# Feed-forward weights issued right behind the last query projection and no longer one by one; one stationary tile for both halves of each down product

## The chip, the cores and the metric

One core of one Trainium2 chip. The time is the device time of an execution in microseconds. PE is TensorE, PEld its weight loads, ACT ScalarE, DVE VectorE, SP the engine that issues most DMAs, in program order. "Half clock" is a stretch in which the records show TensorE's granted clock at 0.5.

## The reference, cut to what matters

A memory-augmented recurrent attention over 64 segments of 32 tokens, then a gated feed-forward. Everything is bfloat16; tokens 2048, width 640, 32 heads of 128, feed-forward width 1728.

```
for s in range(64):                       # each segment needs the memory rows of the one before
    h = concat([mem, x[32*s : 32*s+32]])
    q, k, v = h @ Wq, h @ Wk, h @ Wv
    o = softmax(mask(q k^T * scale)) v @ Wo
    mem = o[:8]; outs.append(o[8:])
h  = x + concat(outs)
n  = layernorm(h)
h2 = h + (relu(n @ W_gate) * (n @ W_up)) @ W_down
```

## The kernel before

A small dependency tracker turns read and write keys into semaphore waits. A write to a key waits for the key's last writer *and* for all its readers since. SP works through its DMAs in program order and blocks at the first that has to wait.

SBUF is nearly full. The gate weights (Wg), the up weights (Wu), their remainder (Wgu, 2 x 64 columns) and the first block of normalized rows (xn2T) take the place of the query weights; Wd, the down weights, and the rows `h` take that of the key weights. `("Wdone", j)` is a key that each projection with weight matrix j writes.

```python
def load_gate_up():
    free = [("W", 0, 0), ("W", 0, 1)]                 # the query weights' keys
    dma(xn2T[0], xn2_d, r=[...] + [("Wdone", 0)], w=[...])
    for n, (t, src) in enumerate(((Wg, B_W_gate), (Wu, B_W_up))):
        dma(t, src[..., 0:FM],             w=free + [(("Wg", "Wu")[n],)])   # each writes `free`,
        dma(Wgu[..., n*FR:(n+1)*FR], src[..., FM:F], w=free + [("Wgu", n)]) # so waits for the last
# ... (cut)
for s in range(NSEG):
    # project K; P.V of segment s-1; project Q (not in the last); project V; scores; softmax  (cut)
    v_riders(par, t0, nr)          # copies of 24 token rows of V between partitions, by DMA
    if s == NSEG - 2:
        load_gate_up()
    # attention output, Wo pass, the attention rows' stores  (cut)
# hand-over: last segment's rest, mixed with gate_up(0, 0..3) on PE
dma(h_rows[0], h_d, ...)
dma(Wd[:, 0:FC-1, :], ..., w=[("W", 1, 0), ("W", 1, 1), ("Wd", 0)])
dma(Wd[FR:128, FC-1, :], ..., w=[("W", 1, 0), ("W", 1, 1), ("Wd", 1)])
for i in range(4, 8): ln2_load(i)                     # eight loads of x and attention rows
trans_ox(s-1); wo_pass(...); rows(...)                # rows: ACT copies to wtok, SP stores it
gate_up(0, 0); pv_x(s); gate_up(0, 1); trans_ox(s); wo_pass(...); rows(...); gate_up(0, 2) # ... (cut)

def down(b, u):                                        # one 128-token tile; contraction 13 x 128 + 64
    for hf in range(2):
        for j in range(FC):                            # FC = 14; the last tile has 64 rows
            p0 = 0 if j < FC - 1 else FR
            pe.matmul(bank(BD[hf])[:, 0:320], hT[par][p0:128, j, u*128:(u+1)*128],
                      Wd[p0:128, j, hf*320:(hf+1)*320], start=(j == 0), stop=(j == FC - 1))
        # DVE: osb = bank + h_rows
```

The softmax here doesn't subtract the row's maximum and nothing guards it: scores larger than these inputs give would overflow.

## Time and profile before

| | before |
|---|---|
| time at the prediction | 1268.34 us, median of 3 (1266.53 to 1270.35) |
| profiled span | 1262.6 us |
| last query projection ends | 1026.65 us |
| first down product starts | 1101.51 us |
| 112 down matmuls of a block, first to last start | 16.72 us |

The page of before, its span, PE's busy share and the chain of work that ended last by engine:

```profile
span 1262.6 us, 64636 instructions
...
PE 1176.5 (93%) x31431; PEld 661.4 (52%) x29111; DVE 611.0 (48%) x1497; ACT 408.4 (32%) x775; POOL 26.6 (2%) x94
...
PE 86%; DMA 4%; DVE 4%; ACT 3%; issue 1%; SPq 1%; POOL 0%; DVEq 0%; ACTq 0%; POOLq 0%
```

PE is the bottleneck, and 4% of the chain is DMA, half of it the loads at the start. The rest lies in the hand-over. The timeline of before, SP's DMA issues there (start, duration of the issue, what is loaded from what):

```profile
1033.95 0.43 SPq L304 DMA_DIRECT2D Wg<-in_B_W_gate_dram  x1
1044.24 0.38 SPq L304 DMA_DIRECT2D Wgu<-in_B_W_gate_dram  x1
1046.34 0.37 SPq L304 DMA_DIRECT2D Wu<-in_B_W_up_dram  x1
1055.37 0.37 SPq L304 DMA_DIRECT2D Wgu<-in_B_W_up_dram  x1
...
1057.96 11.35 SPq L304 DMA_DIRECT2D Wd<-in_B_W_down_dram  x2
...
1075.04 6.17 SPq L304 DMA_DIRECT2D attn_d<-wtok  x12
```

Each weight goes out when the one before has landed; the twelve attention stores stand behind the second piece of Wd. What PE and ACT pay, from the timeline of before (in brackets the idle time ahead of the line and what ended it):

```profile
1055.49 2.29 PE L884 MATMUL ps<-xn2T,Wu 128*128 128x512 bf16 x5 [4.24 <-DMA Wu<-in_B_W_up_dram]
...
1079.37 0.30 ACT L378 ACTIVATE wtok<-ps 128x160 bf16<-128x160 f32 x1 [12.69 <-DMA attn_d<-wtok]
...
1080.22 1.25 PE L884 MATMUL ps<-xn2T,Wg 128*128 128x512 bf16 x5 [3.14 <-ACT g L897]
```

PE's weight loads in a down group, from the timeline of before:

```profile
1248.25 1.85 PEld L912 LDWEIGHTS ps<-Wd,hT 64*128 64x128 bf16 x14 [0.26 <-issue]
...
1250.36 1.85 PEld L912 LDWEIGHTS ps<-Wd,hT 64*128 64x128 bf16 x14 [0.26 <-issue]
```

A group of 14 takes 2.11 us, and there is one break in it, ahead of the 64-row tile.

### The profile page before, as it was taken

What the parts mean: (1) busy time and instruction counts of PE and PEld (TensorE: products, weight loads), DVE (VectorE), ACT (ScalarE), POOL (GpSimd) and SP (SyncE); (2) the same over time, 40 slices, a digit from 0 to 9 for tenths busy, and PEclk for the clock granted to TensorE, in tenths of its full rate; (3) what the DMA queues carried; (4) which work ended last, traced back from release to release, by engine and by line L of the source; (5) the groups of instructions that cost most, each with busy time, mean ns of one, the idle gap of its engine ahead of it and who ended that gap; (6) DMA issues with size and microseconds to landing.
All of it is one profiled execution on the core that took longest, in us unless ns stands there. A gap on an engine that the chain in (4) does not pass through costs nothing.

```text
span 1262.6 us, 64636 instructions
## 1 busy us (share of the span) xinstructions
PE 1176.5 (93%) x31431; PEld 661.4 (52%) x29111; DVE 611.0 (48%) x1497; ACT 408.4 (32%) x775; POOL 26.6 (2%) x94
## 2 busy tenths in 40 slices
PE   0889999999999999999999999999999997999998
PEld 0255555555556555555555555555555554455454
DVE  2244545454545454555555555454545442543522
ACT  0323333333333333333333333333333321321311
POOL 1000000000000000000000000000000000000000
PEclk9999999999999999999999999999999998999999
DMA  9801000010110101010111010100000025110100
GB/s 364 310 21 24 21 23 21 23 23 22 23 24 21 25 19 25 21 44 19 43 22 44 21 44 20 24 20 23 20 21 20 19 99 183 37 63 22 43 21 21
DMA packets 47819, 60.03 MB, mean 48 GB/s; under 512 B 20224, under 2 KB 36288, under 8 KB 47552
## 3 DMA queue, kind: packets, MB, share of 16 engines
q1 hardware_dynamic: 43520, 45.41, 12.6%
q10 hardware_dynamic: 4032, 10.49, 2.2%
q8 instruction: 237, 3.88, 1.3%
q14 instruction: 30, 0.25, 0.1%
HBM read 36.79 MB, written 6.55 MB: 34 GB/s over the span
## 4 chain that ended last, share of the span: by engine, by line
PE 86%; DMA 4%; DVE 4%; ACT 3%; issue 1%; SPq 1%; POOL 0%; DVEq 0%; ACTq 0%; POOLq 0%
PE ps L345 32%; PE ps L546 12%; PE ps L331 9%; PE ps L884 9%; PE ps L364 6%; PE ps L912 5%; PE ps L488 3%; PE ps L372 2%; PE ps L558 2%; PE ps L521 2%; DVE TBf L466 2%; DMA W<-in_A_Wk_dram 2%; PE ps L583 2%; ACT Kr L378 1%; ACT Qr L378 1%
## 5 line engine op out<-in xcount | busy, mean ns | idle before, releaser
L345 PE MATMUL ps<-W,act_r 128*32 128x512 bf16 x6460 | 447.2, 381 | 39.0 <-DVE act_r L467 12.6
L345 PEld LDWEIGHTS ps<-W,act_r 128*32 128x32 bf16 x6460 | 162.9, 96 | 286.0 <-issue 84.4
L380 DVE CAST tok<-ps 128x512 bf16<-128x512 f32 x161 | 110.9, 689 | 154.8 <-PE ps L345 78.3
L378 ACT ACTIVATE tok<-ps 128x512 bf16<-128x512 f32 x161 | 95.9, 596 | 229.7 <-PE ps L331 187.8
L546 PE MATMUL ps<-Wo,oT 128*32 128x160 bf16 x8448 | 163.8, 236 | 3.1 <-issue 2.6
L546 PEld LDWEIGHTS ps<-Wo,oT 128*32 128x32 bf16 x8448 | 148.6, 98 | 12.7 <-issue 4.5
L331 PE MATMUL ps<-W,act_r 128*32 128x512 bf16 x1420 | 138.8, 381 | 0.0
L364 PEld LDWEIGHTS ps<-ident,tok 128*128 128x128 bf16 x1288 | 72.2, 98 | 48.5 <-issue 24.2
L364 PE MATMUL ps<-ident,tok 128*128 128x128 bf16 x1288 | 89.1, 220 | 4.7 <-DVE tok L380 4.7
L604 ACT ACTIVATE oT<-ps 128x768 bf16<-128x768 bf16 x64 | 51.9, 811 | 124.4 <-PE ps L372 124.4
L345 PE MATMUL ps<-W,act_e 128*32 128x512 bf16 x900 | 89.6, 381 | 0.1
L331 PE MATMUL ps<-W,act_e 128*32 128x512 bf16 x900 | 89.2, 379 | 0.0
L378 ACT ACTIVATE Qr<-ps 128x512 bf16<-128x512 bf16 (+3 forms) x110 | 69.1, 658 | 57.4 <-DVE Qr L380 45.4
L596 DVE TENSOR_TENSOR ox<-ps,rx 128x512 bf16<-128x512 f32 x128 | 82.4, 685 | 2.2
L899 DVE TENSOR_TENSOR hT<-g,ps 128x512 bf16<-128x512 bf16 (+1 forms) x56 | 37.8, 686 | 74.7 <-PE ps L884 53.1
L466 DVE STREAM_TRANSPOSE TBf<-ps 128x160 f32<-128x160 f32 x64 | 22.4, 350 | 100.7 <-PE ps L546 100.6
L884 PE MATMUL ps<-xn2T,Wu 128*128 128x512 bf16 x260 | 66.7, 388 | 4.2 <-DMA Wu<-in_B_W_up_dram 4.2
L884 PE MATMUL ps<-xn2T,Wg 128*128 128x512 bf16 x260 | 66.6, 388 | 3.1 <-ACT g L897 3.1
L912 PE MATMUL ps<-Wd,hT 128*128 128x320 bf16 x448 | 68.1, 300 | 0.0
L378 ACT ACTIVATE wtok<-ps 128x160 bf16<-128x160 f32 x64 | 19.5, 304 | 138.7 <-DVE TBf L466 122.4
L897 ACT ACTIVATE g<-ps 128x512 bf16<-128x512 f32 (+1 forms) x56 | 32.3, 594 | 97.1 <-PE ps L884 97.1
L380 DVE CAST Vp<-ps 128x512 bf16<-128x512 f32 x64 | 44.3, 692 | 27.8 <-PE ps L345 26.4
(88 smaller groups left out, 1169.5 us busy)
## 6 DMA issues: line engine op xcount, KB each, us to landing
Vr<-Vp SPq DMA_DIRECT2D x124, 48.8 KB
xt<-in_A_x_dram SPq DMA_DIRECT2D x30, 160.0 KB
Vr<-Vp SPq DMA_DIRECT2D x128, 32.5 KB
attn_d<-wtok SPq DMA_DIRECT2D x256, 7.5 KB
W<-in_A_Wk_dram ACTq DMA_DIRECT2D x1, 2560.0 KB
W<-in_A_Wq_dram ACTq DMA_DIRECT2D x1, 2560.0 KB
W<-in_A_Wv_dram ACTq DMA_DIRECT2D x1, 2560.0 KB
Wo<-in_A_Wo_dram ACTq DMA_DIRECT2D x1, 2560.0 KB
```

Of the source, the lines that this page charges most:

```text
L331: return pe.add_instruction(mybir.InstMatmult(name=nc.get_next_instruction_name(), engine=mybir.EngineType.PE, ins=[pe.lower_ap(rhs), pe.l ...
L345: ins = pe.matmul(*a, start=(c == 0), stop=(c == DC - 1), skip_group_check=True)
L364: ins = pe.matmul(bank_bf(b)[:, k * 128:(k + 1) * 128], t[:, (k % 4) * 128:(k % 4 + 1) * 128], ident[:, :], is_transpose=True)
L378: add("act", lambda a: a.activation(dst, src, ACTF.Copy), r=r, w=w)
L380: add("dve", lambda v: v.tensor_copy(dst, src), r=r, w=w)
L466: add("dve", lambda v: v.transpose(TBf[:].rearrange("p c t -> p (c t)"), src), r=[wkey], w=[("TBf",)])
L488: i = pe.matmul(o, lh, Qr[:, h, q, :], start=True, stop=True, skip_group_check=True)
L546: i = pe.matmul(bank(bk)[32 * gg:32 * gg + 32, 0:160], src[:, hb, :], w[:, gg], start=(hb == 0), stop=(hb == 31), skip_group_check=True)
L596: add("dve", lambda v, kh=kh: v.tensor_tensor(ox[:, :, kh, :], src[:, :, kh, 0:128], ap(rx, kh, [[2, 4], [0, 128]]), ALU.mult), r=[B(b0 + ...
L604: add("act", lambda a: a.activation(oT[par][:, :, M:32].rearrange("p (k g) q -> p g k q", g=4), src[:, :, :, 0:RID], ACTF.Copy), r=[B(bk)] ...
L884: ins = pe.matmul(bank(bk), w[:, c, lo:lo + 128], xn2T[par][:, c, :], start=(c == 0), stop=(c == DC - 1))
L912: i = pe.matmul(bank(bk)[:, 0:320], hT[par][p0:128, j, u * 128:(u + 1) * 128], Wd[p0:128, j, hf * 320:(hf + 1) * 320], start=(j == 0), sto ...
```

## The change

Three parts: the four gate and up weight DMAs wait for the last query projection alone and not for one another, likewise the two of Wd for the last key projection; the gate and up fetch moves from behind segment 62's softmax to right behind its query projection; the two halves of a down product share each stationary tile (`again` issues a matmul without a weight load), in bank pairs that alternate.

```diff
 def load_gate_up():
-    free = [("W", 0, 0), ("W", 0, 1)]
+    free = [("Wdone", 0)]
...
-        dma(t, ..., w=free + [(("Wg", "Wu")[n],)])          # and Wgu alike
+        dma(t, ..., r=free, w=[(("Wg", "Wu")[n],)])
...
             if not last:
                 project(a, ks, 0, (0, 1), (P0, P1))
+                if s == NSEG - 2:
+                    load_gate_up()
...
-        if s == NSEG - 2:
-            load_gate_up()
...
-    dma(Wd[...], ..., w=[("W", 1, 0), ("W", 1, 1), ("Wd", 0)])   # second piece alike
+    dma(Wd[...], ..., r=[("Wdone", 1)], w=[("Wd", 0)])
...
 def down(b, u):
-    for hf in range(2): for j in range(FC): matmul(bank(BD[hf]), hT[j], Wd[j, hf])
+    bks = (BD, BT)[u % 2]
+    for j in range(FC):
+        p0 = 0 if j < FC - 1 else FR
+        for hf in range(2):
+            if hf and not p0: again(pe, ...)                 # no weight load
+            else:             pe.matmul(...)                 # the 64-row tile loads twice
```

More of the change, by code (lines that the diff above doesn't have):

```diff
@@ L327, in build_kernel, with again @@
     nq = [0]
-    def again(pe, dst, lhsT, rhs, start, stop, g):
+    def again(pe, dst, lhsT, rhs, start, stop, g, size=(128, 32)):
         return pe.add_instruction(mybir.InstMatmult(
@@ L333, in again @@
             ins=[pe.lower_ap(rhs), pe.lower_ap(lhsT)], outs=[pe.lower_ap(dst)], start_tensor_calc=start,
-            stop_tensor_calc=stop, tile_size=(128, 32), tile_position=(0, 32 * g), bass_skip_group_check=True, ldweights=False))
+            stop_tensor_calc=stop, tile_size=size, tile_position=(0, 32 * g), bass_skip_group_check=True, ldweights=False))
     def project(act, akeys, j, halves, banks, chunks=range(5)):
@@ L713, in load_gate_up @@
         for n, (t, src) in enumerate(((Wg, B_W_gate), (Wu, B_W_up))):
-            dma(t[:, :, :], src.rearrange("(c p) f -> p c f", p=128)[:, :, 0:FM], w=free + [(("Wg", "Wu")[n],)])
+            dma(t[:, :, :], src.rearrange("(c p) f -> p c f", p=128)[:, :, 0:FM], r=free, w=[(("Wg", "Wu")[n],)])
             dma(Wgu[:, :, n * FR:(n + 1) * FR], src.rearrange("(c p) f -> p c f", p=128)[:, :, FM:F],
-                w=free + [("Wgu", n)])
+                r=free, w=[("Wgu", n)])
     PARTS = ((0, 1), (2, 3), (4,))
@@ L905, in down, with f @@
         n_o[0] += 1
-        for hf in range(2):
-            bk = BD[hf]
-            for lo, hi in ((0, FC - 2), (FC - 2, FC)):
-                def f(pe, hf=hf, bk=bk, lo=lo, hi=hi):
-                    for j in range(lo, hi):
-                        p0 = 0 if j < FC - 1 else FR
-                        i = pe.matmul(bank(bk)[:, 0:320], hT[par][p0:128, j, u * 128:(u + 1) * 128],
-                                      Wd[p0:128, j, hf * 320:(hf + 1) * 320], start=(j == 0), stop=(j == FC - 1))
-                    return i
-                add("pe", f, r=[("hT", par, j) for j in range(lo, hi)] + [("Wd", 0), ("Wd", 1)], w=[B(bk)])
+        bks = (BD, BT)[u % 2]
+        for lo, hi in ((0, FC - 2), (FC - 2, FC)):
+            def f(pe, lo=lo, hi=hi):
+                for j in range(lo, hi):
+                    p0 = 0 if j < FC - 1 else FR
+                    for hf in range(2):
+                        a = (bank(bks[hf])[:, 0:320], hT[par][p0:128, j, u * 128:(u + 1) * 128],
+                             Wd[p0:128, j, hf * 320:(hf + 1) * 320])
+                        if hf and not p0:
+                            i = again(pe, *a, j == 0, j == FC - 1, 0, (128, 128))
+                        else:
+                            i = pe.matmul(*a, start=(j == 0), stop=(j == FC - 1), skip_group_check=True)
+                return i
+            add("pe", f, r=[("hT", par, j) for j in range(lo, hi)] + [("Wd", 0), ("Wd", 1)], w=[B(k) for k in bks])
+        for hf in range(2):
+            bk = bks[hf]
             add("dve", lambda v, hf=hf, bk=bk: v.tensor_tensor(osb[o][:, hf * 320:(hf + 1) * 320], bank(bk)[:, 0:320],
@@ L925, in build_kernel @@
     dma(Wd[:, 0:FC - 1, :], B_W_down[0:FM, :].rearrange("(j p) d -> p j d", p=128),
-        w=[("W", 1, 0), ("W", 1, 1), ("Wd", 0)])
-    dma(Wd[FR:128, FC - 1, :], B_W_down[FM:F, :], w=[("W", 1, 0), ("W", 1, 1), ("Wd", 1)])
+        r=[("Wdone", 1)], w=[("Wd", 0)])
+    dma(Wd[FR:128, FC - 1, :], B_W_down[FM:F, :], r=[("Wdone", 1)], w=[("Wd", 1)])
     for i in range(4, 8):
```

## The prediction

> **What bounds the kernel now.** The page of before: span 1262.6 us, PE busy 93%, the chain that ended last 86% PE. Up to 1030 us that is the attention recurrence, which the change does not touch. It touches two places.
>
> *1. The hand-over to the feed-forward, 1030 to 1085 us.* The chain of waits there is made of DMA. In the timeline SP issues Wg at 1033.95, the next piece at 1044.24, Wu at 1046.34, the last at 1055.37: each write to the same tracking key waits for the landing before it (SP waits: 9.8 us for Wg, 8.7 for Wu). The last query projection, which frees their space, ends at 1026.9. PE pays three times:
> - Gate product 0 is done at 1051.1; PE idles 4.24 us for Wu.
> - The clock records then grant half speed from 1054.3 to 1061.1 (windows: 0.75 over 1056 to 1066). The five Wu products take 2.2 us, not 1.08; the next Wg five the same.
> - Wd's second piece waits 10.3 us for the first in the SP queue, so twelve attention stores go out only at 1075 to 1081. ACT idles 12.7 us for one of them (a wtok buffer), until 1079.37; its relu comes late and PE idles 3.14 us "<-ACT g" before 1080.22. More half clock follows (1081.6 to 1085.0).
>
> *2. The down products.* Four blocks of 112 matmuls take 16.88 us each, 150.7 ns per matmul, at clock 1.00. Start to start most are 135.8 ns, the weight load hidden. The excess is at the last, 64-row tile: 232 ns into it, 238 out of it, 147 for the next, about 0.21 us per group of 14. This agrees with "Mode switching requires drain" (the Trainium skill, TensorEngine Tiling (Array Packing), Key Properties).
>
> **What the change does.** The weights are issued from about 1027.0, when SP has finished its stores, within 2.5 us. The queue moved about 400 GB/s at its peaks, so 5.1 MB should land near 1042, before 1050. The 62nd segment's V rider copies now stand behind them (descriptors are consumed in ring order: DMA: Bandwidth & Descriptors, HWDGE ordering), landing near 1044 by this estimate; they are needed at 1052. Wd goes out near 1041, lands near 1055, is needed past 1085. The attention stores go out near 1050 and land near 1056; ACT needs that at about 1062.
>
> PE then runs Wu at 1051.1, the value product to 1052.95, gate/up 1 to 1055.1. Before, that point was 1061.9: 6.8 us saved. The ACT stall goes, 3.3 us, and the half clock behind it, 1.7 us. Sum 11.8 us, all on the critical path.
>
> Down: dropping 208 of 448 weight loads saves nothing by itself, since they are hidden. But both halves now share one visit to the 64-row tile: 16 groups instead of 32, 16 x 0.21 = 3.4 us. Both evictions now follow the last matmul: the tail grows by one, 0.5 us. Net 2.9 us.
>
> **Prediction.** 1268.3 - 11.8 - 2.9 = 1253.6 us. 8 in 10: 1249.5 to 1258. Faster by over 2%: 0.03; within 2%: 0.96; slower: 0.01.
>
> **What would show it.** No PE wait on DMA Wu; clock 1.00 from 1038 us to the end; no ACT wait over 1 us for an attention store; 112 down matmuls in about 16.0 us, still 136 ns apart; half as many slow steps; PE idle between segments 62 and 63 (om, ox) unchanged.
>
> **What would make it wrong.** Rider copies or stores held behind 9 MB of weights, so that the value product of segment 63 or ACT waits; instruction fetch slowed by the full DMA (two PE gaps of 0.4 to 0.6 us marked "issue" stand here already); a matmul without weight load not streaming at 136 ns.

## More of the kernel before

The stage windows of before, with the granted clock (PEclk), the DMA engines' share and their GB/s. The rows are: query projection to gate product 0; to the last transposes of the attention output; to gate/up 5; to the first down product; one block of down products.

```profile
core 0: us, PE busy (x) PEld busy (x) DVE busy (x) ACT busy (x) POOL busy (x), PEclk, DMA share, GB/s
1026.65:1050.00 23.35, 18.81 (x631) 13.29 (x623) 8.43 (x22) 6.27 (x11) 0.00 (x0) 0.93 0.48 163
1050.00:1061.93 11.93, 7.69 (x89) 2.85 (x86) 2.18 (x4) 1.50 (x3) 0.00 (x0) 0.71 0.62 211
1061.93:1080.22 18.29, 14.59 (x360) 9.18 (x358) 1.67 (x3) 2.54 (x6) 0.00 (x0) 1.00 0.58 182
1080.22:1101.51 21.29, 21.29 (x106) 9.79 (x107) 14.17 (x30) 8.71 (x21) 0.00 (x0) 0.92 0.02 4
1101.51:1118.40 16.89, 16.89 (x115) 10.24 (x112) 4.82 (x9) 1.47 (x3) 0.00 (x0) 1.00 0.09 30
```

The second stage is a third idle and runs at 0.71 of the clock. The down stage is full at full clock; the reader has to look at single starts to see anything there.

## The result, and the profile after

| | before | after |
|---|---|---|
| time, fast runs of the first set | 1267.65 us (4 runs) | 1257.28 us (4 runs) |
| ratio, 95% interval | | 0.9916 (0.9898 to 0.9934) |
| control, second set | 1266.28 us (11 runs) | 1258.89 us (6 runs) |
| ratio, 95% interval | | 0.9940 (0.9918 to 0.9962) |

A ratio compares two kernels in the same set and is not quite the ratio of the medians quoted; a gain in microseconds is here 1 minus the ratio, times the median of before in that set. The gain is 10.6 us by the first set, 7.6 us by the control; 14.7 us were forecast (a ratio of 0.9884, below both intervals). The time lies inside the stated range, but only by 0.7 us, and the control's 1258.89 us lies 0.9 us above it: that the range held is in part luck. "Within 2%" was right.

The profiled spans differ less, 1262.6 and 1258.4 us, because this execution of the changed kernel was 4.7 us later already at the last query projection (1031.38 us), where the two programs are the same. So stages are compared from there. From the last query projection to the first down product it is 74.86 us before and 69.27 after: 5.6 us, of 11.8 forecast.

SP's issues in the timeline of after:

```profile
1031.97 0.43 SPq L304 DMA_DIRECT2D Wg<-in_B_W_gate_dram  x1
1032.44 0.52 SPq L304 DMA_DIRECT2D Wgu<-in_B_W_gate_dram  x1
1033.00 1.16 SPq L304 DMA_DIRECT2D Wu<-in_B_W_up_dram  x1
1034.20 4.38 SPq L304 DMA_DIRECT2D Wgu<-in_B_W_up_dram  x1
1038.62 5.13 SPq L304 DMA_DIRECT2D Vr<-Vp  x4
...
1046.89 3.37 SPq L304 DMA_DIRECT2D Wd<-in_B_W_down_dram  x2
```

They follow at once, as intended (an issue itself now takes up to 4.4 us; why is not shown). No PE or ACT wait names Wu or an attention store any more. But the time did not all come back. PE in the timeline of after:

```profile
1038.09 0.91 PE L546 MATMUL ps<-Wo,oT 128*32 128x160 bf16 x34
1039.62 2.99 PE L546 MATMUL ps<-Wo,oT 128*32 128x160 bf16 x94 [0.62 <-issue]
...
1043.27 2.12 PE L345 MATMUL ps<-W,act_r 128*32 128x512 bf16 x34 [0.66 <-DVE act_r L467]
1045.83 0.61 PE L345 MATMUL ps<-W,act_r 128*32 128x512 bf16 x6 [0.44 <-issue]
...
1054.68 1.35 PE L546 MATMUL ps<-Wo,oT 128*32 128x160 bf16 x66
1058.96 2.21 PE L546 MATMUL ps<-Wo,oT 128*32 128x160 bf16 x62 [2.93 <-issue]
```

Three times PE stops in the middle of a run of equal matmuls, waiting for nothing that the profile shows ("issue"), for 0.62, 0.44 and 2.93 us. In before the third of these places, at the same instructions, has a gap of 0.36 us:

```profile
1047.07 1.35 PE L546 MATMUL ps<-Wo,oT 128*32 128x160 bf16 x66
1048.78 1.28 PE L546 MATMUL ps<-Wo,oT 128*32 128x160 bf16 x62 [0.36 <-issue]
```

The stage windows of after, for the same five stages:

```profile
1031.38:1061.50 30.12, 21.63 (x630) 14.31 (x624) 8.44 (x22) 6.57 (x12) 0.00 (x0) 0.85 0.94 316
1061.50:1066.88 5.38, 5.22 (x82) 2.49 (x83) 2.18 (x4) 1.20 (x3) 0.00 (x0) 0.90 0.04 9
1066.88:1081.07 14.19, 13.71 (x357) 9.23 (x359) 2.83 (x5) 3.64 (x7) 0.00 (x0) 1.00 0.04 8
1081.07:1100.65 19.58, 19.48 (x104) 9.35 (x105) 13.10 (x28) 7.63 (x19) 0.00 (x0) 1.00 0.01 3
1100.65:1116.60 15.95, 15.95 (x115) 5.47 (x60) 4.04 (x8) 1.47 (x3) 0.00 (x0) 1.00 0.09 32
```

The second to fourth stages gained 6.55 + 4.10 + 1.71 = 12.4 us, a little more than forecast. The first lost 6.8 us, 23.35 to 30.12, with the DMA engines 0.94 busy and the clock at 0.85. The down block gained 0.94 us. Its weight loads now, from the timeline of after:

```profile
1245.59 0.10 PEld L917 LDWEIGHTS ps<-Wd,hT 128*128 128x128 bf16 x1 [0.17 <-issue]
1246.09 0.11 PEld L917 LDWEIGHTS ps<-Wd,hT 64*128 64x128 bf16 x2 [0.40 <-issue]
1246.46 0.25 PEld L917 LDWEIGHTS ps<-Wd,hT 128*128 128x128 bf16 x2 [0.26 <-issue]
```

The break at the 64-row tile comes once in 28 matmuls (4.01 us), not in 14.

### The profile page after: what moved, and what is told of

Same layout as the page of the kernel before. It is cut to its first block, busy times and chain, and to the rows that moved or that the text cites. A ratio compares the mean times of both kernels' runs of the same rounds, so it can differ in the third digit from the quotient of the medians.

```text
span 1258.4 us, 64411 instructions
## 1 busy us (share of the span) xinstructions
PE 1171.8 (93%) x31413; PEld 642.5 (51%) x28903; DVE 609.7 (48%) x1497; ACT 408.2 (32%) x775; POOL 26.5 (2%) x94
## 3 DMA queue, kind: packets, MB, share of 16 engines
q1 hardware_dynamic: 43520, 45.41, 12.7%
HBM read 36.79 MB, written 6.55 MB: 34 GB/s over the span
## 4 chain that ended last, share of the span: by engine, by line
PE 89%; DVE 4%; ACT 3%; issue 2%; DMA 2%; POOL 0%; SPq 0%; DVEq 0%; POOLq 0%
PE ps L345 33%; PE ps L546 13%; PE ps L331 11%; PE ps L884 9%; PE ps L364 7%; PE ps L917 3%; PE ps L488 3%; PE ps L372 2%; PE ps L558 2%; PE ps L521 2%; PE ps L583 2%; DVE TBf L466 2%; DMA W<-in_A_Wk_dram 2%; ACT Kr L378 1%; ACT Qr L378 1%
## 5 line engine op out<-in xcount | busy, mean ns | idle before, releaser
L345 PE MATMUL ps<-W,act_r 128*32 128x512 bf16 x6460 | 449.9, 382 | 41.0 <-DVE act_r L467 12.7
L546 PEld LDWEIGHTS ps<-Wo,oT 128*32 128x32 bf16 x8448 | 148.8, 98 | 16.3 <-issue 7.9
L884 PE MATMUL ps<-xn2T,Wg 128*128 128x512 bf16 x250 | 63.0, 381 | 1.6 <-issue 1.4
L884 PE MATMUL ps<-xn2T,Wu 128*128 128x512 bf16 x254 | 63.3, 379 | 0.3
L917 PE MATMUL ps<-Wd,hT 128*128 128x320 bf16 (+1 forms) x240 | 63.3, 300 | 0.0
```

What stands on the lines that cost most here:

```text
L345: ins = pe.matmul(*a, start=(c == 0), stop=(c == DC - 1), skip_group_check=True)
L546: i = pe.matmul(bank(bk)[32 * gg:32 * gg + 32, 0:160], src[:, hb, :], w[:, gg], start=(hb == 0), stop=(hb == 31), skip_group_check=True)
L884: ins = pe.matmul(bank(bk), w[:, c, lo:lo + 128], xn2T[par][:, c, :], start=(c == 0), stop=(c == DC - 1))
L917: i = pe.matmul(*a, start=(j == 0), stop=(j == FC - 1), skip_group_check=True)
```

## A theory, and its rivals

**Theory F.** The Trainium skill (Runtime: NRT & Kernel Launch, Instruction fetch mechanics) says that an engine's instruction memory is refilled in blocks of 16 KiB, 256 instructions, over a DMA queue, and that crossing a boundary is "mostly hidden". The trace has such a queue; the page of after lists its packets, their MB and their share of the DMA engines' time (each packet has 16,384 bytes):

```profile
q8 instruction: 236, 3.87, 1.3%
```

I counted PE's matmuls, weight loads and semaphore instructions from the start of the trace. Of all gaps over 0.3 us without a wait after the first 72 us, all 7 of before and all 15 of after stand at instruction number 193 or 194 modulo 256:

```
before: 209.4 (1.27 us)  582.2  644.8  833.9  896.3  1048.8 (0.36)  1069.4 (0.57)
after:  148.1  210.1 (1.25 us)  241.6  272.3  523.7  585.9  698.6  837.9  869.9  900.2  962.3  1024.5
        1039.6 (0.62)  1045.8 (0.44)  1059.0 (2.93)
```

So PE stood waiting for its next block. At such a gap the last fetch packet usually starts about 2 us before PE stops; for the gap of 2.93 us it starts 0.4 us *after* PE had stopped. The theory: the fetch shares the 16 DMA engines with the weights, and stands behind them.

The packets of all 14 traces ("before" to "d1" in the table below) show it more exactly. At each of the 141 gaps over 0.3 us at block boundaries PE goes on 2.2 to 3.1 us after the start of the fetch packet, and nowhere earlier than 2.15 us. The packet itself starts a median of 0.8 us and at most 2.2 us after PE has passed the boundary before, where other traffic is under 100 GB/s; beside traffic of over 300 GB/s in rows of 3328 bytes or more it starts 1.5 to 5.0 us after (21 cases, median 3.4). So a gap comes where PE executes a block in less time than the two delays add up to, and traffic lengthens the first.

The gaps of this kind before the query projection, 3.2 us in before and 6.3 in after, make 3.1 of the 4.7 us by which the two executions differ there.

**Rival S.** The new order in SP's queue costs the time: rider copies and stores behind 9 MB of weights. **Rival N.** The profiled run was an odd one. **Rival P.** The gaps belong to the program at that place (the Wo pass, an unseen semaphore), not to the traffic.

The table has for each experiment the time from the last query projection to the first down product ("hand-over"), the sum of PE's gaps over 0.25 us at block boundaries in it, and the time at half clock in it, from one profile each. (The instruction numbers there run from 190 to 194; a few matmul records are missing.)

| kernel | ratio to before (95%) | hand-over us | fetch gaps us | half clock us |
|---|---|---|---|---|
| before | 1 | 74.86 | 0.93 | 13.7 |
| e1 down only | 0.9972 (0.9954 to 0.9989) | 71.06 | 1.31 | 6.8 |
| e2 fetch only | 0.9963 (0.9948 to 0.9979) | 69.67 | 6.08 | 6.8 |
| e3 Wd keys only | 0.9979 (0.9957 to 1.0001) | 71.78 | 2.64 | 6.8 |
| after | 0.9916 (0.9898 to 0.9934) | 69.27 | 3.99 | 10.2 |
| after, control | 0.9940 (0.9918 to 0.9962) | 68.43 | 4.65 | 6.8 |
| e4 early, one by one | 0.9905 (0.9888 to 0.9923) | 65.21 | 3.31 | 0 |
| e6 late, all at once | 0.9932 (0.9911 to 0.9954) | 67.04 | 3.21 | 6.8 |
| v2 Wd deferred | 0.9915 (0.9892 to 0.9939) | 66.00 | 1.54 | 10.2 |
| v4 deferred and paced | 0.9916 (0.9892 to 0.9940) | 64.46 | 1.19 | 6.8 |
| v5 deferred, small rows | 0.9887 (0.9867 to 0.9906) | 62.29 | 1.06 | 0 |
| v6 paced, small rows | 0.9901 (0.9880 to 0.9921) | 64.09 | 1.50 | 3.4 |
| v7 after, small rows | 0.9929 (0.9908 to 0.9950) | 67.40 | 2.80 | 6.8 |
| d1 before with copies | one execution | 71.85 | 0.47 | 10.2 |

Whole times of one kernel vary by 2 to 9 us between executions, as much as the effects here. So the traces carry the mechanism, and the ratios only the larger differences.

The hand-overs of this table mix two things. Take the fetch gaps away, in the kernels where PE waits for no weight or store (for e4 also its 1.15 us for a rider copy), and 60.8 and 61.2 us are left without half clock, 62.6 with 3.4 us of it, 63.3 to 64.6 with 6.8, and 64.5 and 65.3 with 10.2. By these numbers a microsecond at half clock costs about 0.4 us (an estimate). The half clock does not go with the sum of the gaps: e4 has 3.31 us of gaps and none of it, v2 1.54 and 10.2. What sets it is not shown, so a difference between two hand-overs counts for theory F only as far as the gaps column differs too.

## The experiments

### e1: the down product alone

```diff
 # before, plus `again(..., size)` and the new down()
```

> The kernel before with the down product's part of the change alone. From the two traces (a block's 112 matmuls 16.72 to 15.81 us from first to last start, four blocks; the end from the last matmul to the end of the span 3.48 to 3.88 us) it should give 3.3 us, a ratio of 0.9974, if the two parts add. If the missing 4 us of the prediction were lost in the down part, it would give 0 or less.

Measured: 1265.49 us against 1268.12, ratio 0.9972, 3.5 us. In its trace each block takes 15.81 us (16.72 before), and the end of the span comes 4.17 us after the last down matmul starts (3.78). So 157.30 us from first to last down matmul became 153.61: 3.69 us, less 0.39 us at the end, where the last store is issued 1.25 us after the last matmul starts and not 0.86, behind two evictions: 3.30 us. The 153.61 us stand, to 0.01 us, in every kernel that has this part. The shortfall isn't here.

A second finding: its hand-over has before's code and took 71.06 us, not 74.86. The waits of before are in it too (4.35 us for Wu), but the one behind ACT cost PE 1.7 us and not 3.1, and half clock lasted 6.8 us and not 13.7. d1 below, with the same code again, took 71.85. The profile that the prediction was drawn from was 2.3 us above the mean of the three (72.6).

### e2: the weight fetch alone

```diff
 # after, with the old down()
```

> The changed kernel with the old down product: the weight fetch's part alone. If the parts add: 10.5 - 3.3 = 7.2 us, ratio 0.9943, against the 11.8 us that were forecast for it. Theory F (PE's instruction fetch is held up behind the weights on the DMA engines): PE gaps marked 'issue' of over 0.5 us between the query projection and gate/up 1 appear here as in the changed kernel, at PE instruction numbers that are a multiple of 256 apart, with the fetch's packets starting late. Rival N (the profiled run of after was just an odd one): no gap over 0.6 us.

Measured: ratio 0.9963, 4.7 us, less than the 7.2 expected, but with e1's 3.5 us it makes 8.2, between the two results for the whole change (10.6 and 7.6). Its trace has the three fetch gaps at the same places, 1.00, 1.60 and 3.48 us; at the last the fetch packet started 0.9 us after PE had stopped. Rival N falls: the gaps are in all three profiles that have this fetch.

### e3: Wd's keys alone

```diff
 # before
-    dma(Wd[...], ..., w=[("W", 1, 0), ("W", 1, 1), ("Wd", 0)])
+    dma(Wd[...], ..., r=[("Wdone", 1)], w=[("Wd", 0)])          # second piece alike
```

> The kernel before with only the two down-weight loads no longer waiting for one another. By the prediction's account the attention stores then go out 10 us earlier, ACT's 12.7 us wait and PE's 3.14 us before 1080.22 go, and the half clock behind it: 5.0 us, ratio 0.9961; the 4.24 us for Wu stay. If the stores stay late because the ring is full of weights, less than 2 us.

Measured: ratio 0.9979, 2.7 us of the 5.0 expected, and the interval just includes no change. In its trace the stores go out from 1070.7 us; ACT waits 7.7 us for one, not 12.7, and none of it reaches PE. In their place PE has a fetch gap of 2.28 us in the Wo pass that now meets the traffic of Wd (0.47 to 1.31 us there in the three profiles with before's code). The wait for Wu was 6.7 us in this profile.

### e4: early, but one by one

```diff
 # after
 def load_gate_up():
-    free = [("Wdone", 0)]; ... r=free, w=[...]
+    free = [("W", 0, 0), ("W", 0, 1)]; ... w=free + [...]
```

> The changed kernel, the gate and up weights fetched behind the last query projection but again one by one; all else as in the changed kernel. From before's spacings they then land 10.3, 12.4, 21.4 and about 23 us after the query projection, just as Wu is needed. Theory F: fewer bytes stand in front of the instruction fetch, each PE gap at a multiple of 256 instructions stays under 1 us, and it is 1 to 4 us faster than the changed kernel (ratio 0.988 to 0.991), unless the rider copies, now issued at about +23 us, come late for the value product. Rival S (the order and back-pressure of the SP queue cost the time): SP is blocked longer here, so it is slower than the changed kernel (ratio over 0.992).

Measured: ratio 0.9905, 12.0 us, as expected of theory F and against rival S, although SP is blocked until 22 us after the query projection here and PE waits 1.15 us for a rider copy. The fetch gaps are not all smaller and the expected 1 us is just missed (1.00, 1.04, 1.27 us), but none is over 1.3 us, and the clock stayed full. By its interval it is not shown to be faster than the changed kernel in time; in the trace its hand-over is 3.2 to 4.1 us shorter, most of it, by the estimate above, from the absent half clock: the gaps are only 0.7 and 1.3 us less.

### e6: late, but all at once

```diff
 # after, with load_gate_up() called behind v_riders() as before
```

> The changed kernel, the gate and up weights issued at the old place (behind the rider copies, about 7 us after the query projection) but not one by one. From the 400 GB/s seen, 5.1 MB land about 21 to 22 us after the query projection, before Wu is needed at about 24: the 4.2 us wait for Wu goes without the move. Theory F: PE's fetch gaps of over 1 us move with the traffic, to the block boundaries at about +14 and +22 to +28 us, and the time is within 3 us of the changed kernel. Rival: the earlier issue is what matters, then PE waits for Wu again and it is 4 us slower than the changed kernel.

Measured: ratio 0.9932, between the two results of the changed kernel, and no PE wait for Wu. The largest fetch gap, 2.08 us, now stands 23.8 us after the query projection, as expected; the one expected at about +14 did not come. With e4 this says that either the move or the free issue removes the wait for Wu; together they add nothing that these runs can show.

### d1: copies in the middle of the recurrence

```diff
 # before
             v_riders(par, t0, nr)
+            dump(s)    # s = 18, 36: one DMA of 2.1 MB, Wo in SBUF to a scratch tensor in DRAM, 3328-byte rows
+                       # s = 24, 42: two of them at once;  s = 30, 48: one of 2.1 MB in 512-byte rows
```

> The kernel before with copies of the output-projection weights from SBUF to a scratch tensor in DRAM added in the middle of the recurrence, which nothing waits for: segments 18 and 36 one of 2.1 MB in 3328-byte rows, 24 and 42 two of 2.1 MB at once, 30 and 48 one of 2.1 MB in 512-byte rows. Theory F: PE gaps without a wait appear in the 6 to 12 us behind each, at the same instruction numbers modulo 256, 0.5 to 1 us for one copy and 1 to 3 us for two; none of that size in the segments without copies. Rival (the gaps belong to the hand-over's own program, such as the Wo pass with its bank or an unseen semaphore): no gaps in those segments beyond the 0.4 to 1.3 us that appear in one segment of nine anyway.

The result stays correct; the scratch tensors are read by nobody. SP and PE around the copy of segment 18, from the timeline of d1:

```profile
350.35 0.45 SPq L304 DMA_DIRECT2D dump<-Wo  x1
...
356.62 0.39 PE L331 MATMUL ps<-W,act_r 128*32 128x512 bf16 x3
358.63 0.38 PE L331 MATMUL ps<-W,act_r 128*32 128x512 bf16 x1 [1.62 <-issue]
```

and the two copies of segment 24:

```profile
451.30 0.38 PE L345 MATMUL ps<-W,act_r 128*32 128x512 bf16 x2
453.97 0.39 PE L345 MATMUL ps<-W,act_r 128*32 128x512 bf16 x2 [2.29 <-issue]
```

| copy issued at | size, rows | traffic | fetch gaps while it ran and just after |
|---|---|---|---|
| 350.4 | 2.1 MB, 3328 B | about 400 GB/s | 1.62 us |
| 641.3 | 2.1 MB, 3328 B | about 400 GB/s | 1.01 us at 649.5, 0.58 at 657.0 |
| 445.6 | 4.3 MB, 3328 B | about 390 GB/s | 2.29 us |
| 737.1 | 4.3 MB, 3328 B | about 390 GB/s | 0.47 us, and 2.49 at 753.7 |
| 545.8 | 2.1 MB, 512 B | about 290 GB/s | none for 46 us, with a fetch at 552.4 |
| 833.5 | 2.1 MB, 512 B | about 290 GB/s | none for 18 us, with fetches at 836.3 and 842.3 |

All stand at 193 or 194 modulo 256. Traffic that nothing waits for stops PE, far from the hand-over and in other groups of matmuls (projections). Rival P falls. The gaps of the single copies are longer than expected. One expectation was too strong: gaps of 0.9 to 1.2 us also stand at 210.1, 592.7, 852.4 and 914.7 us, in segments without a copy. And there was a surprise: the same bytes in 512-byte rows caused no gap. But they did delay the fetch: its packets started 4.4 us (545.8), 1.8 and 3.6 us (833.5) after PE had passed the boundary before, against 3.9 to 5.0 us behind the copies in 3328-byte rows. At 545.8 PE found no gap because it spent 6.7 us on that block, and 3.4 to 5.8 us on the blocks that ended in the gaps of the table. So d1 alone does not show that small rows spare the fetch.

### after_again, v2 and v4: the traffic moved away from PE's dense instruction streams

> The changed kernel unaltered, as the control of this set: 1257 us, ratio 0.990 to 0.993. Theory F: its second profile again shows PE gaps without a wait after the query projection, at PE instruction numbers a multiple of 256 apart, adding to 3 to 6 us, the largest about 27 us after the query projection.

The control: ratio 0.9940, just outside the expected 0.990 to 0.993; gaps 2.15 us at +14.5 and 2.19 us at +27.9 us after the query projection, 4.65 us in all.

```diff
 # v2: after, with h rows and Wd moved from the start of the hand-over
     gate_up(0, 3)
+    dma(h_rows[0], ..., r=[..., ("Wdone", 1), ("hT", 0, 3)]); dma(Wd ...); dma(Wd ...)   # same added key
```

> The changed kernel with the h rows and the down weights (2.9 of the 9.2 MB) issued only after gate/up 3. Theory F: the queue is then empty by about 22 us after the query projection, so the largest PE gap (2.9 and 3.5 us at +27 us in the changed kernel and in the fetch part alone) falls below 0.6 us, with the half clock behind it; 3 to 5 us faster than the control. Rival S (order of the SP queue) or chance: no change over 1 us, since nothing that PE waits for by semaphore is moved earlier.

Measured: the gap at +27 us, found in after, e2 and the control, is gone; what is left is 0.47 and 1.07 us. Hand-over 66.0 us against the control's 68.4, although half clock lasted 10.2 us here and 6.8 there. The medians differ by 2.5 us (1256.37 and 1258.89), the intervals overlap. Nothing that PE waits for by semaphore was moved earlier, which rival S would need.

```diff
 # v4: v2, with Wu and its remainder behind v_riders() and waiting for Wg
+        r=[("Wdone", 0), ("Wg",)]
```

> As the last, and Wu with its remainder issued behind the rider copies and only when Wg has landed, so never more than about 2.8 MB stand in the ring. Theory F: the gap at +14.5 us shrinks too; PE gaps after the query projection add to under 2 us; 4 to 6 us faster than the control, ratio to before 0.985 to 0.988, and no PE wait for a rider copy. If the paced kernel is no better than the deferred one, the depth of the ring matters less than whether it is busy at all.

Measured: fetch gaps 1.19 us (0.65 and 0.54), as expected, no wait for a rider copy, hand-over 64.5 us, but the ratio, 0.9916, is that of v2. Of the 4 to 6 us expected over the control about 3 are seen, by the medians.

### v5, v6 and v7: the same bytes in 512-byte rows

```diff
 # v5 on v2, v6 on v4, v7 on after
-        dma(t[:, :, :], src[..., 0:FM], ..., w=[(("Wg", "Wu")[n],)])
+        for lo in range(0, FM, 256):
+            hi = min(FM, lo + 256)
+            dma(t[:, :, lo:hi], src[..., lo:hi], ..., w=[(("Wg", "Wu")[n], lo)])
```

> The kernel with deferred down weights, its gate and up weights fetched in pieces of 256 columns, so that every packet is 512 bytes and not 3328. In the dump run 3328-byte packets held PE's fetch up by 1.0 to 2.5 us and 512-byte packets by nothing over 0.25 us. If packet size is what matters: both gaps (0.47 at +8.5 and 1.07 at +15 us) fall under 0.3 us, the traffic runs at about 290 GB/s, the weights land about 20 us after the query projection, and it is 1 to 2 us faster from query projection to first down product than the deferred kernel (66.0 us). If only the amount of data in flight matters, the gaps stay.

Measured: 1252.89 us against 1267.38, ratio 0.9887, 14.3 us: by its ratio the fastest kernel, though the intervals of e4 and v6 overlap its own. Its interval lies below the control's and overlaps that of the first set of after by 0.0008. The same three block boundaries as in after, from the timeline of v5:

```profile
1040.96 1.84 PE L546 MATMUL ps<-Wo,oT 128*32 128x160 bf16 x94 [0.18 <-issue]
...
1045.80 0.61 PE L345 MATMUL ps<-W,act_r 128*32 128x512 bf16 x6 [0.23 <-issue]
...
1055.48 1.28 PE L546 MATMUL ps<-Wo,oT 128*32 128x160 bf16 x62 [1.06 <-issue]
```

0.62, 0.44 and 2.93 us became 0.18, 0.23 and 1.06. The last came with only some 45 GB/s of other traffic, and is of the kind that the recurrence has anyway: the packet started 1.2 us after the boundary before, as in quiet stretches, but PE executed that block in 2.8 us. The clock stayed full from the query projection to the last matmul. Its hand-over is 3.7 us shorter than that of v2, more than the 1 to 2 us expected; the gaps make 0.5 us of it, and v2's 10.2 us at half clock, by the estimate above, the rest. Of the gain 0.7 us is at the very end: the span ends 3.48 us after the last down matmul starts, not 4.17, in all three kernels with small rows. That need not be due to the rows: d1, which has large ones, has 3.30 where before has 3.78.

> The paced kernel with the same 512-byte packets. If packet size is what matters, its two gaps (0.65 and 0.54 us) go and it takes 63 to 64.5 us from query projection to first down product (64.5 in the paced kernel); 12 us faster than before, ratio 0.988 to 0.992. It may lose if Wu, fetched at 290 GB/s behind Wg, lands after about +24 us.

Measured: ratio 0.9901; hand-over 64.1 us, gaps 0.46 and 1.05. Hand-over and ratio are as expected, but the two gaps did not go, and pacing on top of small rows gives nothing.

> The changed kernel with one edit: the gate and up weights in pieces of 256 columns, 512-byte packets for 3328. The down weights stay where the change put them. If the way the gate and up weights are packed held up PE's fetch: no gap over 0.5 us at +8.5 and +15 us (0.6 and 0.4, none and 2.1, 1.0 and 1.6 us in the three profiles so far), while the gap at +22 to +28 us, which falls in the down weights' 1280-byte packets, stays at 1 to 3.5 us; query projection to first down product 65 to 68 us, against 68.4 to 69.7. If packing does not matter, both gaps stay and the time is that of the changed kernel.

Measured: the one-edit test on the changed kernel itself. It was run on another chip. PE in the timeline of v7:

```profile
1035.76 1.84 PE L546 MATMUL ps<-Wo,oT 128*32 128x160 bf16 x94 [0.18 <-issue]
...
1040.60 0.61 PE L345 MATMUL ps<-W,act_r 128*32 128x512 bf16 x6 [0.22 <-issue]
...
1061.55 1.25 PE L546 MATMUL ps<-Wo,oT 128*32 128x160 bf16 x31 [2.23 <-issue]
```

The gaps at the block boundaries expected at +8.5 and +15 us are 0.18 and 0.22 us; the gap in Wd's 1280-byte rows stays, 2.23 us at +33.5 us (the traffic there has moved: 358 to 383 GB/s from +28). The fetch for the first two starts 2.4 us after the boundary before, for 2.6 to 4.2 us in after and the control. Hand-over 67.4 us, inside the expected 65 to 68. The ratio, 0.9929, is that of the changed kernel: the gaps are 1.2 and 1.9 us less than in its two profiles, the hand-over 1.9 and 1.0 us, too little to show in times that vary by 6 us.

**What stays open.** 512-byte rows also move fewer bytes per second (about 290 GB/s for 400). Whether the size of a row or the rate decides was not separated. The page on DMA (DMA: Bandwidth & Descriptors, Queues, rings and completion order) says that an engine changes queues only between packets; that would fit, but no run shows it by itself. The gaps with little traffic need no late fetch: at the 117 of them over 0.3 us PE had executed the block in 2.6 to 3.7 us, about what the two delays add up to without traffic. That the packet stands behind the weights in the engines' queues is argued: the traces show when it starts, not when it was asked for. What starts a stretch of half clock stays open.

## Why the prediction was right or wrong

*Right:*

- **The down product.** Forecast 3.4 us less 0.5, net 2.9; measured 3.69 less 0.39, 3.30 us. Matmuls without a weight load still start 136 ns apart, and the slow steps are one visit to the 64-row tile per 28 matmuls. This agrees with "Mode switching requires drain" (the Trainium skill, TensorEngine Tiling (Array Packing), Key Properties): saving 208 of 448 weight loads left the 136 ns as they were; halving the 32 visits, at about 0.21 us each, gives 3.4 us of the 3.69.
- **The waits that go.** PE's 4.24 us for Wu, ACT's 12.7 us and PE's 3.14 us behind it are gone in after, and nothing waits for a rider copy. The stages behind gate product 0 gained 12.4 us.
- **The kind of risk.** The last paragraph of the prediction named instruction fetch under full DMA.

*Wrong, step by step:*

- **"PE then runs Wu at 1051.1", "Sum 11.8 us".** The Wu products started 31.5 us after the query projection, not 24.4. The prediction left the first stage, up to gate product 0, as it was; it grew by 6.8 us. The term that was left out of the sum is the growth of PE's waiting for its next 256 instructions: 4.0, 4.7 and 6.1 us in the three profiles with this fetch, 0.5 to 1.3 us in those with before's.
- **"Clock 1.00 from 1038 us to the end".** After has half clock for 3.4 us each at +17.5 and +27.7 us, the control for 6.8 us at +16.3. The Trainium skill (TensorE: Matmul & The Clock Gate, Part 1) tells of a free-running window of about 3.4 us by which PE's activity sets its clock to full or half; the records here agree, they are stretches of 3.413 us or twice that, but whether a stretch follows a gap changes from run to run. So this term cannot be taken from one trace. It is as large as the first: by the estimate of 0.4 us per microsecond, the 10.2 us at half clock in the hand-over of after cost about 4 us.
- **The base.** 1.7 us for one half clock and 2.3 us above the mean hand-over were in the one profile that the forecast was counted on. From the mean, 72.6 us, to the forecast end, 63.1 us, only 9.5 us were to be had.

The forecast end was no fiction: v5, with the same waits gone and fetch gaps of 1.06 us, has a hand-over of 62.29 us and a time of 1252.89 us, against 63.1 and 1253.6 forecast for the change. By profiles the change got 72.6 - 69.3 = 3.3 us in the hand-over, about 9.5 forecast from that base; the difference is the fetch gaps and the half clock. An estimate from the table adds up: the forecast end keeps before's 0.9 us of fetch gaps and its first 3.4 us at half clock; after has 4.0 and 10.2 us, so 3.1 us of gaps and 0.4 x 6.8 = 2.7 us of half clock more, 5.8 of the 6.2 us by which its hand-over misses 63.1 us. By times, after less the down part is 7.3 us in the first set and 4.3 in the control; with 2 to 9 us between executions, these runs don't fix it closer.

## What to carry to other kernels

A load that nothing waits for still is not free: PE's instructions arrive by DMA too, and where a stretch of short matmuls eats 256 instructions in under about 6 us, loads at 400 GB/s stopped it here. So issue large loads early enough, but no more at once than is needed, into stretches of long matmuls, and try smaller rows (in v7 they closed two gaps of three; its time did not show it); and look for PE gaps marked "issue" at a fixed distance in instructions. For a small gain, count from the mean of several profiles: one profile holds half-clock stretches that the next does not.

## What the Trainium skill lacked or had wrong

- **Runtime: NRT & Kernel Launch, Instruction fetch mechanics:** 16 KiB blocks of 256 instructions agree with the trace, and so does "mostly hidden": of some 230 boundaries after the first 72 us, 7 in before and 15 in after have a gap over 0.3 us. The page does not say what those cost (4.1 and 10.3 us in all, up to 3.5 us for one in e2), nor that other DMA traffic delays the fetch; 2.1 MB in 3328-byte rows at 400 GB/s made gaps of 1.0 and 1.6 us.
- **DMA: Bandwidth & Descriptors:** it has no figure for how long a small transfer of another queue stands behind a stream of rows. The fetch packets started 1.5 to 5.0 us after the boundary before beside rows of 3328 bytes or more at over 300 GB/s, 1.3 to 4.4 us beside 512-byte rows, and 0.8 us (median) in quiet. Rows of 512 bytes ran at about 290 GB/s for 400. Nor did I find SP's own time behind a queue of loads: 4.38 us to issue an 80 KB load that takes 0.37 us otherwise.
- **DMA: Bandwidth & Descriptors, Bandwidth:** it says that about 358 GB/s from HBM binds a load; the rows and weights moved at 380 to 410 GB/s over 12 us in after (packets counted in slices of 2 us, rider copies included). The same section explains the difference: 358 GB/s is for two cores that stream at once, and its table for one core reaches 425.
- **TensorEngine Tiling (Array Packing), Key Properties:** it gives no cost for a mode switch; here 232 ns into a 64-row tile and 238 ns out, for 136.
- **TensorE: Matmul & The Clock Gate, Part 2 (Back-to-back issue gap):** a sustained 131 ns per 512-column matmul was not seen; 135 gate and up products in a row took 28.93 us from first to last start in before, 215.9 ns each, at clock 1.00. Its other figure, N / 2.4 + 2.5 ns, gives 135.8 ns for 320 columns, which is what the trace has.
